# Paired blocks of a GELU feed-forward: where the GELU tiles start, and 512-column products cut in two

## The chip, the cores and the metric

One core of one Trainium2 chip runs the whole program. The metric is device time in microseconds (us). The kernel before takes 477.94 us, the median of 3 runs (477.3 to 478.46). The profiled execution shown below took 477.47 us, of which 475.9 us are the span of its instructions, so 1.57 us lie around the span.

## The reference

A gated linear attention (a state of 48 x 48 per head that decays by alpha and takes up k v at each of 768 steps, for 4 batches and 8 heads) makes x of 3072 tokens by 384. Then comes the feed-forward part, which is all that the change touches:

```
h = x @ w_in                                  # 384 -> 2048
g = 0.5 * h * (1.0 + erf(h * inv_sqrt2))      # GELU
return (g @ w_out).astype(np.float32)         # 2048 -> 384
```

## The kernel before

Every fp32 operand of the feed-forward part is held as two tiles of a shorter format (fp32r), a high part and the rest: `x` (both parts in one tile), `wih`/`wil` of w_in, `woh`/`wol` of w_out, `ghi`/`glo` of the GELU. A product of two fp32 blocks is then three products on TensorE: high by high, high by rest, rest by high. In every one of them the stationary operand is 128 x 128 and loaded anew, and the moving operand has 256, 384 or 512 columns. A matmul row of the trace is one such product.

The tokens go in blocks. While the attention part still runs, blocks are narrow (256 tokens): `gemm1` (L682) has 256 moving columns of `x`, `gemm2` (L918) has 384 moving columns of w_out. Later blocks are wide (512 tokens, `WIDE`): `wide1` (L698) has 512 moving columns of `x` in 9 products for each 128 rows f of w_in's output, `wide2` (L713) has 512 moving columns of `ghi` or `glo`.

In the last three wide blocks most steps are paired (`QUICK`: 7, 8 and 7 pairs, 22 in all). A pair takes two f at once. Its two `wide1` are 18 products of 512 columns. Its second GEMM has two halves:

- `quick1` (L806, by `three_terms`): the last 128 of the 384 outputs directly, 6 products with 512 moving columns of GELU (into `acc[2]`); then three blocks of a 2 x 2 scheme with seven block products in place of eight, each with 256 moving columns of one half of a GELU tile, 9 products.
- `quick2` (also recorded at L806): the other four block products, whose moving operands are combinations of GELU halves, 12 products of 256 columns. The combinations are made by VectorE (DVE) at L790 to L796, split into high and rest by ScalarE (ACT) at L799 and by DVE at L802. The trace names the high tile `qd` and the rest `ad`, after the buffers that they reuse.

The stationary operands of the block products are parts of `woh`/`wol`, or sums and differences of such parts, which lie in reused buffers (`x`, `sums_x`, `sums_kn`, `qd`, `kd` and others in the trace).

ACT makes `ghi` (GELU with the output rounded, L893) and the whole GELU `h` (L898); DVE makes `glo` = h - ghi (L908). The tiles of `ghi` and `glo` come from `gelu_tile`: for every second step of the paired stretch from a ring of two buffers (`own` is None), for the others in turn from a third buffer and from the buffers `ghi_vn`/`glo_vn`.

Where a tile starts in a partition, modulo 256 bytes, is set by constants and by filler tiles (`gap`):

```
GELU_AT, HELD_AT, COMB_AT, WIDE_AT, NARROW_AT = 0, 0, 192, 0, 192
```

So before the change all GELU tiles, all weights, their sums and the wide `x` start at 0 modulo 256; the narrow `x` and the tiles of the combinations at 192. Halves and columns within a tile are whole multiples of 256 bytes further on, so a product's moving and stationary operands keep the start of their tiles modulo 256.

The order of the instructions on each engine is written out by a planner that simulates the engines with the costs in `COST` (`quick1`, `quick2`, `low` and so on). It lets a pair's two `wide1` run before the `quick1` and `quick2` of the pair before it: `quick1` waits for the `glo` of its second step, `quick2` for the rest tile of the combinations.

Of the kernel before, what the change touches and what calls it, by code (L numbers as in the profile page):

```python
# [9 lines left out]
F32R = mybir.dt.float32r  # L10
# [34 lines left out]
    wide1=2.1, wide2=2.07, wpart=1.1, quick1=2.45, quick2=1.42, comb1=0.36, comb3=1.08, chi=0.98, clo=1.2, wsum=0.72, wcomb=0.52, whi=0.52, wlo=0.65, gather=1.7, keep=0.95, evac=1.45, wend0=1.38, wend1=2.76, fsum=0.4, fall=0.2, fout=0.2,  # L45
)
LINE = 256
GELU_AT, HELD_AT, COMB_AT, WIDE_AT, NARROW_AT = 0, 0, 192, 0, 192
ORDER = "0 1 a b c 2 d 3 e f 4 g h i j k 5 l m n o p"


# [1 line left out]
def gla_then_gelu_ffn(ctx: ExitStack, tc: tile.TileContext, q, k, v, alpha, qg, kg, ag, vg, w_in, w_out, out):  # L53
    nc = tc.nc
    B, H, D, S = q.shape
    NF, P, NK, _ = w_in.shape
    DM, DFF = NK * P, NF * P
    NT = B * S
    C = 128
    G = 2 * C  # L60
# [7 lines left out]
    NF2 = NF // 2  # L68
# [10 lines left out]
    def gap(pool, size):  # L79

        if size % LINE:
            n = f"gap{len(gaps)}"
            gaps.append(pool.tile([C, size % LINE // 4], F32, tag=n, bufs=1, name=n))

    const = ctx.enter_context(tc.tile_pool(name="const", bufs=1))
    work = ctx.enter_context(tc.tile_pool(name="work", bufs=3))
    ffn = ctx.enter_context(tc.tile_pool(name="ffn", bufs=2))
# [5 lines left out]
    first = first_cm.__enter__()  # L93
# [27 lines left out]
    W = 2 * G  # L121
# [50 lines left out]
    def data_tile(n, i, dtype=F32):  # L172
        return const.tile([P, NPAIR, G], dtype, tag=f"{n}d{i}", name=f"{n}d{i}")
# [3 lines left out]
    for i in range(NB):  # L177
        vbuf.append(const.tile([P, NCH, HV * D + DR], F32, tag=f"vn{i}", name=f"vn{i}"))
        data.append({})
        for n in "akq":  # L180
            if (n, i) in (("q", 0), ("a", 1)):
                gap(const, (COMB_AT - HELD_AT) * (i == 0))
            data[i][n] = data_tile(n, i)
            if (n, i) == ("a", 1):
                gap(const, HELD_AT - COMB_AT)
# [7 lines left out]
    for half in range(2):  # L193
# [6 lines left out]
            base=0,  # L200
# [1 line left out]
            channel_multiplier=-1,  # L202
        )

    wi_hi, wi_lo, wo_hi, wo_lo = (
        [const.tile([P, 2, DM], F32R, name=f"{n}{f2}") for f2 in range(NF2)] for n in ("wih", "wil", "woh", "wol")
    )

    def gelu_minus(hp, ghi):
        h = hp.rearrange("p a t -> p (a t)")  # L210
        nc.tensor.matmul(h, lhsT=minus, rhs=ghi.rearrange("p a t -> p (a t)"), start=False, stop=True, skip_group_check=True)

    def gelu_rest(hp):
        glo = ffn.tile([P, 2, G], F32R, tag="glo", name="glo")
        nc.scalar.copy(glo, hp)
        return glo

    parts_all = const.tile([P, NSB, 2, DM], F32, name="parts")
    parts = [parts_all[:, i] for i in range(NSB)]
    LONG = NK * 2 * G  # L220

    def long_tile(pool, name, **kw):
        return pool.tile([P, LONG + LINE // 4], F32R, name=name, **kw)

    def narrow_x(t):
        at = (NARROW_AT - HELD_AT) % LINE // 4
        return t[:, at : at + LONG].rearrange("p (n h t) -> p n h t", n=NK, h=2)

    x0_room = long_tile(const, "x0")
    x0 = narrow_x(x0_room)  # L230

# [4 lines left out]
    late = []  # L236
# [339 lines left out]
    def block_of(g):  # L576
        return next((pair for pair in WIDE if g in pair), g)

    later = []

    def x_pool():
        if not later:
            early_cm.__exit__(None, None, None)
            later.append(ctx.enter_context(tc.tile_pool(name="later", bufs=1)))
            gap(later[0], WIDE_AT - GELU_AT)
        return later[0]

    def two_x():
        if len(later) < 2:
            later.append(x_pool().tile([P, 2 * LONG + LINE // 4], F32R, name="two_x"))  # L590
        return later[1]

    def both_x(at):
        at = (at - WIDE_AT) % LINE // 4
        return two_x()[:, at : at + 2 * LONG]

    def x_tiles(g):
        pair = block_of(g)
        if pair == g:
            if g == NSB:  # L600
                x = narrow_x(long_tile(late[0], f"x{g}", tag="xn", bufs=1))
                gap(late[0], WIDE_AT - HELD_AT)
            else:
                x = x0 if g in (0, "s") else both_x(NARROW_AT).rearrange("p (g n h t) -> p g n h t", g=2, n=NK, h=2)[:, g - 1]
            xt[g] = x[:, :, 0], x[:, :, 1]
            return x
        if pair not in xt:
            if pair == WIDE[2]:
                x = both_x(WIDE_AT).rearrange("p (n j h t) -> p n j h t", n=NK, j=2, h=2)
            else:  # L610
                x = late[0].tile([P, NK, 2, 2, G], F32R, tag="xl", name=f"x{g}")
            xt[pair] = x
        h = pair.index(g)
        return xt[pair][:, :, h]
# [189 lines left out]
    def three_terms(to, a, b, start):  # L804
        for n, (x, y) in enumerate(((0, 0), (1, 0), (0, 1))):
            nc.tensor.matmul(to, lhsT=a[x], rhs=b[y], start=(start and n == 0), stop=True, skip_group_check=True)  # L806

    def quick1(f2, acc, gs, first, fresh):
        half = [[[x[:, i] for x in g] for i in range(2)] for g in gs]
        whole = [[x.rearrange("p a t -> p (a t)") for x in g] for g in gs]  # L810
        w = [[[x[:, j, e * P : (e + 1) * P] for x in (wo_hi[f2], wo_lo[f2])] for e in range(3)] for j in range(2)]
        s4 = [x[:, 1] for x in sums[f2]]
        three_terms(acc[2], w[0][2], whole[0], first)
        three_terms(acc[2], w[1][2], whole[1], False)
        three_terms(sbank[:, 0, :G], w[0][0], half[0][0], fresh)
        three_terms(acc[0][:, :G], w[1][0], half[1][0], first)
        three_terms(acc[0][:, G:], s4, half[1][1], False)
# [56 lines left out]

    own_g = {}

    def gelu_tile(n, own):

        if own is None:
            return ffn.tile([P, 2, G], F32R, tag=n, bufs=2, name=n)  # L880
        if (n, own) not in own_g:
            if own:
                i = int(n == "glo")
                t = const.tile([P, NCH, HV * D + DR], F32R, tag=f"vn{i}", name=f"{n}_vn").rearrange("p j e -> p (j e)")
                at = (GELU_AT - (HELD_AT, COMB_AT)[i]) % LINE // 4
                own_g[n, own] = t[:, at : at + W].rearrange("p (a t) -> p a t", a=2)
            else:
                own_g[n, own] = ffn.tile([P, 2, G], F32R, tag=f"{n}3", bufs=1, name=n)
        return own_g[n, own]

    def gelu_high(hp, own=None):
        ghi = gelu_tile("ghi", own)
        nc.scalar.activation(ghi, hp, AF.Gelu)  # L893
        return ghi

    def gelu_whole(hp, half=None):
        h = hp if half is None else work.tile([P, 2, G], F32, tag=("fl", "kx")[half], bufs=1, name="h")
        nc.scalar.activation(h, hp, AF.Gelu)  # L898
        return h

    def gelus(g, f, hp):
        ghi = gelu_high(hp)
        gelu_whole(hp)
        return ghi

    def gelu_low(g, f, hp, ghi, own=None):
        glo = gelu_tile("glo", own)
        nc.vector.tensor_tensor(out=glo, in0=hp, in1=ghi.bitcast(F32), op=ALU.subtract)  # L908
        return glo

# [327 lines left out]

    total = const.tile([P, 1], F32, name="total")
    flag = const.tile([1, 1], I32, name="flag")  # L1240
    gap(const, -64)
    gap(ffn, GELU_AT - HELD_AT)

    def flag_sum():
        nc.vector.tensor_scalar(
# [148 lines left out]
    def gemm1_op(g, t):  # L1394
        f = next_f[g]
        next_f[g] += 1
        st = dict(g=g, f=f, first=g != state["g"], last=False)
# [12 lines left out]
        fast = g in QUICK and f // 2 in QUICK[g]  # L1410
        if fast and not state["more"]:
            assert unit[n_units - 1]["mask"].end is not None and unit[n_units - 1]["mask"].end <= t
            state["more"] = 1
            state["count"] = 0
        own = None
        if state["more"]:
            m = state["count"]
            own = None if m % 2 else m // 2 % 2
            two = steps[-4] if m > 2 else steps[-3] if m == 1 else {}
            state["count"] += 1  # L1420
# [9 lines left out]
            st["gemm1"] = Op("PE", "wide1" if wide else "gemm1", lambda: st.update(hp=(wide1 if wide else gemm1)(g, f)))  # L1430
        past = steps[-2] if fast and "pair" in steps[-2] else None
        room_free = two.get("frees", two.get("gemm2"))
        st["high"] = Op("ACT", "gelu", lambda: st.update(gh=gelu_high(st["hp"], own)), [st["gemm1"], room_free], rank=-3)
        st["gelu"] = Op("ACT", "gelu", lambda: st.update(h=gelu_whole(st["hp"], f % 2 if fast else None)), [st["high"], past and past["low"], past and past.get("c3")], rank=-3)
        if len(steps) < STEPS_BY_PRODUCT:
            st["minus"] = Op("PE", "gminus", lambda: gelu_minus(st["hp"], st["gh"]), [st["gelu"]], rank=-2)
            st["low"] = Op("ACT", "rest", lambda: st.update(gl=gelu_rest(st["hp"])), [st["minus"], room_free], rank=-3)
            waiting["PE"].append(st["minus"])
        else:
            st["low"] = Op("DVE", "low", lambda: st.update(gl=gelu_low(g, f, st["h"], st["gh"], own)), [st["gelu"], room_free], rank=-3)  # L1440

        def second(which):
            if "acc" in st:
# [165 lines left out]
    t = 0.0  # L1609
    idle = 0  # L1610
    while True:
# [17 lines left out]
        t = min(later_on)  # L1629
# [92 lines left out]
```

## Time and profile before

| what | value |
|---|---|
| median of 3 runs | 477.94 us |
| profiled execution | 477.47 us |
| its span | 475.9 us |
| TensorE (PE) busy | 466.1 us, 98% |
| weight loads (PEld) busy | 411.2 us, 86% |
| DVE busy | 340.6 us, 72% |
| ACT busy | 230.6 us, 48% |
| granted TensorE clock | full, mean 0.996 |

PE is busy from about 50 us to its last product at 469.2 us. A matmul row gives the start and a modelled duration, which holds the way through the array; products that follow each other overlap in it. How fast TensorE takes them is therefore read from the distance between starts.

### The profile page before, as it was taken

Reading aid. Unit: us, or ns where it says so; the run is one execution under the profiler, and the core shown is the slowest. Engines: PE = TensorE matmul, PEld = TensorE weight load, DVE = VectorE, ACT = ScalarE, POOL = GpSimd, SP = SyncE. Lnnn points to the kernel's source line nnn. Section 1 sums busy time; section 2 is a strip of 40 time slices with the busy share of each in tenths; the row PEclk is TensorE's granted clock in tenths of the full one; section 3 lists DMA queues with packets and bytes.
Section 4 is the critical chain, followed back from the end, with each engine's and each line's share of the span. In section 5 each row is a group of like instructions: output and inputs, shape, how many; then the busy total and the mean of one; then the engine's idle time right before and its main releaser. Section 6 shows DMA issues by size and latency. Waiting matters only on the chain.

```text
span 475.9 us, 12527 instructions
## 1 busy us (share of the span) xinstructions
PE 466.1 (98%) x5328; PEld 411.2 (86%) x5328; DVE 340.6 (72%) x666; ACT 230.6 (48%) x429; POOL 7.4 (2%) x21
## 2 busy tenths in 40 slices
PE   8999999999999999999999999999999999999994
PEld 5788999999999999887888878888888888888883
DVE  6999999987977978788992365887575454745442
ACT  4898676454544344535433345454444343534340
POOL 2000000000000000000000000000000000000000
PEclk9999999999999999999999999999999999999998
DMA  8997655556756654646340031000010000010002
GB/s 298 401 392 259 234 168 163 165 179 179 213 157 195 209 168 154 205 139 211 117 148 0 22 137 33 1 0 2 0 68 0 1 0 1 23 45 0 1 1 74
DMA packets 33920, 56.67 MB, mean 119 GB/s; under 512 B 3744, under 2 KB 13280, under 8 KB 33856
## 3 DMA queue, kind: packets, MB, share of 16 engines
q1 hardware_dynamic: 32400, 50.94, 32.3%
q0 software_dynamic: 880, 3.93, 2.1%
q8 instruction: 44, 0.72, 0.6%
q10 hardware_dynamic: 576, 0.92, 0.6%
q14 instruction: 20, 0.16, 0.1%
HBM read 43.45 MB, written 12.32 MB: 117 GB/s over the span
## 4 chain that ended last, share of the span: by engine, by line
PE 91%; DMA 4%; DVE 3%; issue 1%; ACT 0%; SPq 0%; DVEq 0%; ACTq 0%
PE hw L698 28%; PE acc L918 13%; PE hp L682 13%; PE accw L806 11%; PE accw L713 9%; PE sbank L806 6%; PE sbank L482 2%; DMA st<-in_moe_w_out_dram 2%; PE sbank L559 2%; PE sbank L501 2%; DMA two_x<-zd 1%; PE sh L392 1%; DVE pp L352 1%; DMA ad<-in_ag_dram 0%; DVE rp L365 0%
## 5 line engine op out<-in xcount | busy, mean ns | idle before, releaser
L698 PE MATMUL hw<-x,wih 128*128 128x512 f32 x288 | 89.2, 391 | 0.0
L893 ACT ACTIVATE ghi<-hw 128x512 fp32r<-128x512 f32 x53 | 31.7, 599 | 70.1 <-PE hw L698 70.1
L698 PEld LDWEIGHTS hw<-x,wih 128*128 128x128 f32 x288 | 52.9, 188 | 10.4
L698 PE MATMUL hw<-x,wil 128*128 128x512 f32 x144 | 56.2, 390 | 0.0
L802 DVE TENSOR_TENSOR ad<-ad,qd 128x1024 fp32r<-128x1024 f32 x22 | 26.9, 1224 | 32.1 <-ACT qd L799 32.1
L799 ACT CAST qd<-ad 128x1024 fp32r<-128x1024 f32 x22 | 23.1, 1051 | 47.3 <-PE accw L806 47.3
L918 PE MATMUL acc<-woh,ghi 128*128 128x384 f32 x128 | 43.9, 343 | 0.0
L918 PE MATMUL acc<-wol,ghi 128*128 128x384 f32 x128 | 43.0, 336 | 0.0
L908 DVE TENSOR_TENSOR glo<-h,ghi 128x512 fp32r<-128x512 f32 x33 | 22.8, 692 | 28.0 <-ACT h L898 28.0
L893 ACT ACTIVATE ghi<-hp 128x512 fp32r<-128x512 f32 x32 | 19.1, 598 | 41.8 <-PE hp L682 41.7
L365 DVE TENSOR_TENSOR_SCAN rp<-ad,rp,bottom 128x255 f32<-128x255 f32 x48 | 34.2, 740 | 0.9
L682 PE MATMUL hp<-two_x,wih 128*128 128x256 f32 x192 | 33.5, 278 | 1.1 <-DMA two_x<-zd 1.1
L682 PE MATMUL hp<-x,wih 128*128 128x256 f32 x192 | 33.9, 279 | 0.0
L352 DVE TENSOR_TENSOR_SCAN pp<-ad,bottom 128x256 f32<-128x256 f32 x48 | 30.7, 668 | 3.4 <-DMA ad<-in_ag_dram 3.4
L698 PEld LDWEIGHTS hw<-x,wil 128*128 128x128 f32 x144 | 27.0, 188 | 5.7
L682 PEld LDWEIGHTS hp<-two_x,wih 128*128 128x128 f32 x192 | 29.5, 188 | 1.2 <-issue 1.2
L698 PE MATMUL hw<-two_x,wih 128*128 128x512 f32 x96 | 29.6, 390 | 0.0
L682 PEld LDWEIGHTS hp<-x,wih 128*128 128x128 f32 x192 | 29.4, 188 | 0.2
L918 PE MATMUL acc<-woh,glo 128*128 128x384 f32 x128 | 28.3, 342 | 0.0
L908 DVE TENSOR_TENSOR glo<-hw,ghi 128x512 fp32r<-128x512 f32 x20 | 13.8, 689 | 20.3 <-ACT hw L898 20.0
L682 PE MATMUL hp<-two_x,wil 128*128 128x256 f32 x96 | 26.6, 277 | 0.0
L682 PE MATMUL hp<-x,wil 128*128 128x256 f32 x96 | 26.4, 277 | 0.0
(282 smaller groups left out, 1120.5 us busy)
## 6 DMA issues: line engine op xcount, KB each, us to landing
st<-in_moe_w_in_dram SPq DMA_DIRECT2D x8, 768.0 KB, 7.4
st<-in_moe_w_out_dram SPq DMA_DIRECT2D x8, 768.0 KB, 6.2
qd<-in_qg_dram SPq DMA_DIRECT2D x23, 256.0 KB, 3.5
ad<-in_ag_dram SPq DMA_DIRECT2D x23, 256.0 KB, 3.3
kd<-in_kg_dram SPq DMA_DIRECT2D x23, 256.0 KB, 4.9
vn<-in_vg_dram SPq DMA_DIRECT2D x12, 416.0 KB, 6.5
fd<-fl SPq DMA_DIRECT2D x18, 256.0 KB, 2.1
kx<-fd SPq DMA_DIRECT2D x72, 64.0 KB, 2.9
```

The costliest lines, as they stand in the source:

```text
L352: nc.vector.tensor_tensor_scan(pp[:, i], at[:, i], bottom, MID, ALU.mult, ALU.max)
L365: nc.vector.tensor_tensor_scan(rp[:, i, G - 2 :: -1], at[:, i, G - 1 : 0 : -1], bottom[:, 1:], rp[:, i, G - 1 :], ALU.mult, ALU.max)
L482: nc.tensor.matmul(ybank[o, i, j * CS : (j + 1) * CS], lhsT=vn[r, j, e : e + rows], rhs=d["ss"][r, h, j, :], start=(j == 0 and i not in sp ...
L682: nc.tensor.matmul(hp[:, j, :], lhsT=a[:, j, i * P : (i + 1) * P], rhs=x[:, i, :], start=(start and m == 0), stop=(stop and (j, i, n) in t ...
L698: nc.tensor.matmul(hp, lhsT=a[:, j, i * P : (i + 1) * P], rhs=x[:, i, :, part], start=(i == 0 and n == 0), stop=(i == NK - 1 and n == 2),)
L713: nc.tensor.matmul(acc[i], lhsT=w[:, j, e], rhs=a, start=(f == 0 and k == 0 and w is wo_hi[f2]), skip_group_check=mixed, stop=(f == NF - 1 ...
L799: nc.scalar.copy(quick["hi"], quick["t"])
L802: nc.vector.tensor_tensor(out=quick["lo"], in0=quick["t"], in1=quick["hi"].bitcast(F32), op=ALU.subtract)
L806: nc.tensor.matmul(to, lhsT=a[x], rhs=b[y], start=(start and n == 0), stop=True, skip_group_check=True)
L893: nc.scalar.activation(ghi, hp, AF.Gelu)
L908: nc.vector.tensor_tensor(out=glo, in0=hp, in1=ghi.bitcast(F32), op=ALU.subtract)
L918: nc.tensor.matmul(acc[t], lhsT=a[:, j, t * C : (t + 1) * C], rhs=w[:, j, :], start=(first and j == 0 and k == 0 and w is wo_hi[f]), stop= ...
```

## The change

GELU tiles of paired steps start at 192 modulo 256 bytes; those of all other steps still start at 0 (`FIRST_GELU_AT`), save where an unpaired step falls to a buffer that only knows the new place (one step at the very end). To this end the ring of two becomes two tiles with a little room, in which a step takes the place it wants. The six products of 512 columns in `quick1` become twelve of 256. Sums of weights stay at 0 modulo 256, and so do the weights of both GEMMs (the fillers are set for it); the buffers that hold sums become 64 bytes shorter. `minus` and `products`, used in a few products at the start, move to 192.

```
-GELU_AT, HELD_AT, COMB_AT, WIDE_AT, NARROW_AT = 0, 0, 192, 0, 192
+GELU_AT, W_IN_AT, WIDE_AT, COMB_AT, HELD_AT, NARROW_AT, FIRST_GELU_AT = 192, 0, 0, 192, 0, 192, 0
...
 def quick1(f2, acc, gs, first, fresh):
     half = [[[x[:, i] for x in g] for i in range(2)] for g in gs]
...
-        three_terms(acc[2], w[0][2], whole[0], first)
-        three_terms(acc[2], w[1][2], whole[1], False)
+        for i in range(2):
+            for j in range(2):
+                three_terms(acc[2][:, i * G : (i + 1) * G], w[j][2], half[j][i], first and i == j == 0)
...
-    def gelu_tile(n, own):
+    def gelu_tile(n, own=None, at=FIRST_GELU_AT):
 
         if own is None:
-            return ffn.tile([P, 2, G], F32R, tag=n, bufs=2, name=n)
+            k = own_g[n] = own_g.get(n, 1) ^ 1
+            base = HELD_AT if n == "ghi" else GELU_AT
+            most = max((x - base) % LINE // 4 for x in (FIRST_GELU_AT, GELU_AT))
+            t = ffn.tile([P, W + most], F32R, tag=f"{n}{k}", bufs=1, name=n)
+            at = (at - base) % LINE // 4
+            return t[:, at : at + W].rearrange("p (a t) -> p a t", a=2)
...
+        at = GELU_AT if fast else FIRST_GELU_AT
...
-        st["high"] = Op("ACT", "gelu", lambda: st.update(gh=gelu_high(st["hp"], own)), [st["gemm1"], room_free], rank=-3)
+        st["high"] = Op("ACT", "gelu", lambda: st.update(gh=gelu_high(st["hp"], own, at)), [st["gemm1"], room_free], rank=-3)
```

The planner's costs and rules are as before, and ACT, DVE, SP and POOL have the same instructions in the same order. Only PE's list differs, in every one of the 22 pairs.

PE before, the second pair's `quick1` from its first product (`accw2` is `acc[2]`, `ghi_vn`/`glo_vn` the GELU of the pair's first step, `ghi`/`glo` of its second, numbers are buffers):

```order
L806 MATMUL accw2_6_4291<-ghi_vn_4463,woh2_136 128x512
L806 MATMUL accw2_6_4291<-ghi_vn_4463,wol2_144 128x512
L806 MATMUL accw2_6_4291<-glo_vn_4469,woh2_136 128x512
L806 MATMUL accw2_6_4291<-ghi_4488,woh2_136 128x512
L806 MATMUL accw2_6_4291<-ghi_4488,wol2_144 128x512
L806 MATMUL accw2_6_4291<-glo_4493,woh2_136 128x512 [waits DVE_49]
L806 MATMUL sbank_80<-ghi_vn_4463,woh2_136 128x256
```

PE now, the same place:

```order
L811 MATMUL accw2_6_4292<-ghi_vn_4465,woh2_136 128x256
L811 MATMUL accw2_6_4292<-ghi_vn_4465,wol2_144 128x256
L811 MATMUL accw2_6_4292<-glo_vn_4471,woh2_136 128x256
L811 MATMUL accw2_6_4292<-ghi_4496,woh2_136 128x256
L811 MATMUL accw2_6_4292<-ghi_4496,wol2_144 128x256
L811 MATMUL accw2_6_4292<-glo_4501,woh2_136 128x256 [waits DVE_49]
```

The six rows now take the first half of each tile, and the same six names follow once more for the second half before `sbank` comes. The wait for DVE's `glo` still stands before the sixth product, which now has only products of 256 columns ahead of it.

PE now, where that pair's `quick1` ends and `quick2` begins (`x0` and `sums_x` hold sums of weights):

```order
L811 MATMUL accw0_6_4290<-ghi_4496,x0_151 128x256
L811 MATMUL accw0_6_4290<-ghi_4496,sums_x_3440 128x256
L811 MATMUL accw0_6_4290<-glo_4501,x0_151 128x256
L811 MATMUL sbank_80<-qd0_4444,x0_151 128x256 [waits Activation_49]
L811 MATMUL sbank_80<-qd0_4444,sums_x_3440 128x256
L811 MATMUL sbank_80<-ad1_4445,x0_151 128x256 [waits DVE_49]
```

These rows stand as they stood before; only the first three read their moving operand from 192 in place of 0.

## Rows read from the trace of the kernel before

**Rows 1.** The page: busy time by engine, PE and its clock in 40 slices
```profile
PE 466.1 (98%) x5328; PEld 411.2 (86%) x5328; DVE 340.6 (72%) x666; ACT 230.6 (48%) x429; POOL 7.4 (2%) x21
...
PE   8999999999999999999999999999999999999994
...
PEclk9999999999999999999999999999999999999998
```

**Rows 2.** Busy time by stretch: stretch, length, then busy us of PE, PEld, DVE...
```profile
195.70:295.40 99.70, 99.70 (x1218) 79.82 (x1218) 66.77 (x148) 43.21 (x88) 1.29 (x2) 1.00 0.35 113
295.40:465.40 170.00, 170.00 (x975) 149.81 (x974) 100.82 (x193) 73.58 (x118) 1.08 (x2) 1.00 0.03 11
```

**Rows 3.** The chain that ended last, paired blocks: start us, length us, what
```profile
299.44 4.09 PE hw L698 x18
303.54 1.36 PE accw L806 x6
...
305.97 1.04 PE sbank L806 x9
...
457.57 4.09 PE hw L698 x18
```

**Rows 4.** Timeline of PE, one pair: start us, duration us, instruction
```profile
437.79 0.39 PE L806 MATMUL accw<-ghi,woh 128*128 128x512 f32 x1
...
438.92 0.39 PE L806 MATMUL accw<-glo,woh 128*128 128x512 f32 x1
439.15 0.28 PE L806 MATMUL sbank<-ghi,woh 128*128 128x256 f32 x1
439.26 0.28 PE L806 MATMUL sbank<-ghi,wol 128*128 128x256 f32 x1
...
440.22 0.40 PE L806 MATMUL sbank<-qd,sums_x 128*128 128x256 f32 x2
...
440.58 0.39 PE L806 MATMUL sbank<-qd,sums_x 128*128 128x256 f32 x2
...
441.60 0.39 PE L698 MATMUL hw<-x,wih 128*128 128x512 f32 x1
```

**Rows 5.** Groups by form, PE: line, names, shapes, count | busy us, mean ns
```profile
L806 PE MATMUL accw<-glo,woh 128*128 128x256 f32 x22 | 6.2, 283 | 0.0
L806 PE MATMUL accw<-qd,woh 128*128 128x256 f32 x22 | 6.1, 276 | 0.0
```

**Rows 6.** The chain again, narrow blocks
```profile
68.68 4.08 PE hp L682 x36
...
89.63 4.17 PE acc L918 x24
```

**Rows 7.** Timeline of PE where a narrow block turns from L918 to L682
```profile
93.63 0.39 PE L682 MATMUL hp<-x,wih 128*128 128x256 f32 x2
93.86 0.28 PE L682 MATMUL hp<-x,wil 128*128 128x256 f32 x1
93.97 0.39 PE L682 MATMUL hp<-x,wih 128*128 128x256 f32 x2
```

**Rows 8.** Timeline of DVE and ACT around the same pair
```profile
431.20 0.69 DVE L908 TENSOR_TENSOR glo<-h,ghi 128x512 fp32r<-128x512 f32 x1 [1.01 <-ACT h L898]
434.90 1.23 DVE L802 TENSOR_TENSOR ad<-ad,qd 128x1024 fp32r<-128x1024 f32 x1 [2.01 <-ACT qd L799]
...
438.48 0.59 ACT L898 ACTIVATE h<-hw 128x512 f32<-128x512 f32 x1
```

**Rows 9.** Timeline of PE behind the last pair: its first and last product
```profile
465.32 0.39 PE L713 MATMUL accw<-ghi,woh 128*128 128x512 f32 x1
...
469.19 0.39 PE L713 MATMUL accw<-glo,woh 128*128 128x512 f32 x1
```

More of the change, by code (lines that the diff above doesn't have):

```diff
@@ L180, in gla_then_gelu_ffn @@
         for n in "akq":
-            if (n, i) in (("q", 0), ("a", 1)):
-                gap(const, (COMB_AT - HELD_AT) * (i == 0))
+            if (n, i) == ("q", 0):
+                gap(const, COMB_AT - HELD_AT)
             data[i][n] = data_tile(n, i)
@@ L203, in gla_then_gelu_ffn, with weight_tiles @@
         )
-    wi_hi, wi_lo, wo_hi, wo_lo = (
-        [const.tile([P, 2, DM], F32R, name=f"{n}{f2}") for f2 in range(NF2)] for n in ("wih", "wil", "woh", "wol")
-    )
+    def weight_tiles(n):
+        return [const.tile([P, 2, DM], F32R, name=f"{n}{f2}") for f2 in range(NF2)]
+    gap(const, W_IN_AT - HELD_AT)
+    wi_hi, wi_lo = weight_tiles("wih"), weight_tiles("wil")
+    gap(const, HELD_AT - W_IN_AT)
+    wo_hi, wo_lo = weight_tiles("woh"), weight_tiles("wol")
     def gelu_minus(hp, ghi):
@@ L213, in gelu_rest @@
     def gelu_rest(hp):
-        glo = ffn.tile([P, 2, G], F32R, tag="glo", name="glo")
+        glo = gelu_tile("glo")
         nc.scalar.copy(glo, hp)
@@ L222, in long_tile @@
     def long_tile(pool, name, **kw):
-        return pool.tile([P, LONG + LINE // 4], F32R, name=name, **kw)
+        return pool.tile([P, LONG + (NARROW_AT - HELD_AT) % LINE // 4], F32R, name=name, **kw)
     def narrow_x(t):
@@ L589, in two_x @@
         if len(later) < 2:
-            later.append(x_pool().tile([P, 2 * LONG + LINE // 4], F32R, name="two_x"))
+            later.append(x_pool().tile([P, 2 * LONG + (NARROW_AT - WIDE_AT) % LINE // 4], F32R, name="two_x"))
         return later[1]
@@ L601, in x_tiles @@
                 x = narrow_x(long_tile(late[0], f"x{g}", tag="xn", bufs=1))
-                gap(late[0], WIDE_AT - HELD_AT)
+                gap(late[0], WIDE_AT - NARROW_AT)
             else:
@@ L887, in gelu_tile, with gelu_high @@
             else:
+                if n == "ghi":
+                    gap(ffn, GELU_AT - HELD_AT)
                 own_g[n, own] = ffn.tile([P, 2, G], F32R, tag=f"{n}3", bufs=1, name=n)
         return own_g[n, own]
-    def gelu_high(hp, own=None):
-        ghi = gelu_tile("ghi", own)
+    def gelu_high(hp, own=None, at=FIRST_GELU_AT):
+        ghi = gelu_tile("ghi", own, at)
         nc.scalar.activation(ghi, hp, AF.Gelu)
@@ L904, in gelus, with gelu_low @@
         return ghi
-    def gelu_low(g, f, hp, ghi, own=None):
-        glo = gelu_tile("glo", own)
+    def gelu_low(g, f, hp, ghi, own=None, at=FIRST_GELU_AT):
+        glo = gelu_tile("glo", own, at)
         nc.vector.tensor_tensor(out=glo, in0=hp, in1=ghi.bitcast(F32), op=ALU.subtract)
@@ L1240, in gla_then_gelu_ffn @@
     flag = const.tile([1, 1], I32, name="flag")
-    gap(const, -64)
-    gap(ffn, GELU_AT - HELD_AT)
+    gap(const, HELD_AT - NARROW_AT - 64)
     def flag_sum():
@@ L1439, in gemm1_op @@
         else:
-            st["low"] = Op("DVE", "low", lambda: st.update(gl=gelu_low(g, f, st["h"], st["gh"], own)), [st["gelu"], room_free], rank=-3)
+            st["low"] = Op("DVE", "low", lambda: st.update(gl=gelu_low(g, f, st["h"], st["gh"], own, at)), [st["gelu"], room_free], rank=-3)
         def second(which):
```

## The prediction

> **What bounds the kernel now.** I read the page's busy times first: PE is busy for 98% of the span at the full clock, and only its first slice is below 9 tenths but for the tail [rows 1]. Then the busy time by stretch: from 295.40 to 465.40, where the 22 pairs run, PE is busy for 170.00 of 170.00 us, DVE for 100.82 and ACT for 73.58 [rows 2]. No wait of PE stands in this stretch. The chain of waits agrees: pair after pair it goes through 18 products at L698 and 27 at L806, all on PE, and nothing of ACT or DVE lies between [rows 3]. So the end is set by how close TensorE takes its products, and an edit is worth what it changes in the distance between their starts.
>
> That distance is read in two ways. One is the chain: from 299.44 to 457.57 lie 20 pairs, 158.13 / 20 = 7.907 us each, of which the 18 products of `wide1` take 4.09 [rows 3]; 3.81 us are left for the second GEMM. The other is the timeline of one pair, from 437.79 to 441.60, again 3.81 us [rows 4]. It falls in four pieces [rows 4]:
>
> - six products of 512 columns, GELU at 0 modulo 256 bytes, 437.79 to 439.15: 1.36 us, 226.7 ns each;
> - nine of 256 columns, GELU at 0, 439.15 to 440.22: 1.07 us. The first, behind a product of 512, takes 0.11 us, so the other eight take 0.96, which is 120 ns each;
> - the first three of 256 columns with a combination at 192, 440.22 to 440.58: 0.36 us, still 120 ns each;
> - the other nine with combinations at 192, 440.58 to 441.60: 1.02 us, 113.3 ns each.
>
> The same shape, 256 columns with a new 128 x 128 stationary operand each time, thus has two prices in one pair. The groups by form say it again: modelled 283 ns where GELU at 0 moves and 276 ns where a combination at 192 moves, both with `woh` as the stationary operand [rows 5]. What differs is the tile that moves, and by its address that is 0 against 192. The narrow blocks give a third witness with other tiles: `x` at 192 by `wih`/`wil`, 36 products in 4.08 us, 113.3 ns each [rows 6].
>
> **The change part by part.**
>
> *Nine products of 256 columns in `quick1`.* Only their moving tile goes from 0 to 192; their stationary operands stay at 0, as those of the nine cheap products are [rows 4]. I take 113.3 ns: 9 x 113.3 = 1.02 us in place of 1.07, so -0.05 us a pair, -1.1 us over 22 pairs. Bounds: the 120 ns they have now (no gain), and 113.3, the least that the trace has for the shape.
>
> *The first three products of `quick2`.* They start at 192 already and cost 120 ns, and from the fourth on the price is 113.3 [rows 4]. I read this as the end of the switch from 0 to 192, and the nine ahead of them will no longer be at 0. The other switch, from 384 columns at 0 to 256 at 192, has no such start: 93.63, 93.86, 93.97 are two products in 0.23 us and a third in 0.11 [rows 7]. So 3 x 113.3 = 0.34 in place of 0.36: -0.02 us a pair, -0.4 us in all. The other end is no gain, if it is the place of their own tile or bank that costs it.
>
> *Six products of 512 into twelve of 256.* Twelve at 192 are 12 x 113.3 = 1.36 us, as much as the six cost now [rows 4]. So this edit is worth nothing, and is needed only since the GELU tile moves: a 512-column product at 192 stands nowhere in the trace of before. If the twelve cost 120 ns, 1.44 us, it loses 0.08 us a pair, 1.8 us in all. Each of the twelve loads weights anew; the narrow blocks show 36 loads in a row at this distance [rows 6], and a pair now has 33 in a row, so no new run is longer than one that is there.
>
> A rule speaks against the cut. The Trainium skill, TensorE: Matmul & The Clock Gate, section Back-to-back issue gap, puts the isolated distance at the columns over 2.4 GHz plus 2.5 ns, and its section Step-by-step: what each phase is for has weights loaded by a read port of their own; neither has a term for where a tile starts. By that rule each cut costs 2.5 ns, an estimate of 6 x 22 x 2.5 ns = 0.33 us more, and moving the tiles gives nothing. The trace does not agree: one shape has two distances, 120 and 113.3 ns [rows 4], both well over the 109.2 ns that the rule would give.
>
> *What lies beside it.* ACT writes `ghi` and DVE reads and writes GELU tiles at the new place. I have no row for these two operations at 192, but they are off the path by far. The `glo` that the pair at 437.79 waits for is done at 431.20 + 0.69 = 431.89, and the sixth product waits for it at 438.92 [rows 4, 8]. With 256-column products ahead of it, it comes 5 x 113.3 ns = 0.57 us in place of 1.13 us behind the first: 6.4 us of cover in place of 7.0. Behind the waiting product stands all of `quick1`, but nothing makes it wait. The combinations' rest tile is done at 434.90 + 1.23 = 436.13, 4.1 us before its first use group at 440.22, and the bank that `wide1` takes at 441.60 is read for the last time at 438.48 + 0.59 = 439.07 [rows 4, 8]. The pair gets shorter by less than 0.1 us, so 2.5 us stay. Even an ACT or DVE operation of twice the length would be hidden. Cost: nothing.
>
> *Behind the pairs.* The next products at L698 come after a switch from 192 to 0, as they do now. Of the 18 products from 465.32 to 469.19 [rows 9] nine read GELU in a buffer that now starts at 192, with 512 columns. From the nearest rows: 120 - 113.3 = 6.7 ns less, or twice that more, 9 products: -0.06 to +0.12 us. I take 0.
>
> *Room and first products.* The wide and narrow blocks keep their places (0 for 384 and 512 columns, 192 for 256). `minus` and `products` at 192 are used in a few products at the start; nothing.
>
> **The sum.** 22 x (0.05 + 0 + 0.02) = 1.5 us; with the unrounded distances, 7.907 - 4.09 - 33 x 0.1133 = 0.078 us a pair from the chain and 3.81 - 3.74 = 0.07 from the timeline, so 1.5 to 1.7. I take 1.55 us. The profiled execution: 475.9 - 1.55 = 474.35 us of span, and with the 1.57 us around it 475.9. It lay 0.47 us under the median; the median becomes 477.94 - 1.55 = 476.4 us.
>
> **The rivals.**
>
> *The start of quick2 stays at 120 ns.* Then only the nine products gain: -1.1 us, 476.8. For it: the three all go to one part of the combinations, the same in every pair. Against it: the other nine products of the combinations have the low price, and so have the first ones behind 384 columns at 0 [rows 4, 7].
>
> *The low price belongs to the tiles, not to the place.* On the other side: if GELU tiles go on moving at 120 ns wherever they start, twelve products cost 1.44 us in place of 1.36, the nine and the three stay, and each pair gets 0.08 us longer: +1.8 us, 479.7. The place is the block at the head of `quick1`. It decides from the distance s at which 21 s + 0.34 equals 1.36 + 1.07 + 0.36, that is 117 ns. For it: no row of before has GELU moving at 192. Against it: `x` by `wih` and combinations by `woh` share nothing but the place, and both have 113.3 [rows 4, 6].
>
> *Place is worth nothing and a cut is free.* The nine then keep their 1.07 us and the twelve take the 1.36 us of the six, whatever makes the combinations cheaper, and the sum is 0 (477.9). The rule named above would add its estimate to that, 478.3. Against it stand the two distances [rows 4].
>
> *That the change does not do what it says* would need a paired step whose tile stays at 0; by `at = GELU_AT if fast` and the three kinds of buffers all 44 steps of the pairs go to 192, so I give it no chance of its own.
>
> **How the numbers follow.** Forecast 80%, the start of `quick2` staying 9%, no effect 5%, the slower case 6%. The three runs of before lie 1.2 us apart, so a median carries some 0.4 us either way. The bound for a difference is 0.2%, 0.96 us here, about what a measurement of this kernel can tell from no change: faster means under 476.98. The forecast lies 0.58 below that and falls there nine times in ten (0.73 of 0.80), the second case somewhat over half of the time (0.06): 0.79 faster. Same: 0.07 + 0.03 + 0.05 = 0.15. Slower: 0.06. The range runs from the best sum, 1.7 + 0.06 us less, by a median's spread to 475.5, and up to 477.4, which holds the second case whole and leaves out the no-effect and the slower case.
>
> **What would show it.** After: 33 products of 256 columns in a row at L811, 113 to 114 ns apart from the first to the last, 3.74 us for all; no 0.12 at the start of `quick2`; a pair in 7.83 to 7.84 us along the chain; 18 products of `wide1` still in 4.09; PE still without waits between the pairs; modelled durations of 276 in place of 283 for the GELU groups. It would be wrong if GELU groups keep 120 ns, if the twelve take longer than 1.38 us, or if PE waits for `glo` at the sixth product.

## The result and the profile after

The changed kernel takes 479.74 us, the median of 8 runs (478.88 to 481.94), against 477.29 us of 8 runs of before on the same chip: a ratio of 1.0051, 95% interval 1.003 to 1.0072. A second comparison on another chip gave 1.0033 (1.0018 to 1.0049), 480.06 against 478.43 us. Both intervals lie above 1: the change makes the kernel slower, by 0.3 to 0.5%. The forecast was 476.4 us, faster.

The bound is where it was. This is the row of the changed kernel's busy time by stretch that answers to [rows 2]: PE is busy through all of the paired blocks, and no wait of PE stands there. The granted clock (the number before the last two) is 1.00 in that stretch, as it was before, so the clock has no part in what follows.

```profile
295.40:465.40 170.00, 170.00 (x1090) 155.04 (x1089) 101.33 (x195) 74.67 (x119) 1.08 (x2) 1.00 0.03 11
```

The chain of the changed kernel, for [rows 3] (start us, length us, what):

```profile
299.40 1.06 PE sbank L811 x9
...
300.82 4.08 PE hw L703 x18
304.89 1.41 PE accw L811 x12
...
460.15 4.08 PE hw L703 x18
```

From 300.82 to 460.15 lie 20 pairs, 7.967 us each in place of 7.907. The twelve cut products take 1.41 us (the six took 1.36 and the forecast was 1.36). And the nine products of `quick2` in `sbank`, which the change does not touch, take 1.06 us where they took 1.04 with three dear ones at their head [rows 3]. The timeline of one pair shows the distances, for [rows 4] (start us, duration us):

```profile
304.73 0.28 PE L811 MATMUL accw<-ghi_vn,woh 128*128 128x256 f32 x1
304.85 0.28 PE L811 MATMUL accw<-ghi_vn,wol 128*128 128x256 f32 x1
...
307.21 0.28 PE L811 MATMUL sbank<-qd,x 128*128 128x256 f32 x1
...
307.56 0.28 PE L811 MATMUL sbank<-qd,x 128*128 128x256 f32 x1
...
308.62 0.61 PE L703 MATMUL hw<-x,wih 128*128 128x512 f32 x2
```

From 304.73 to 308.62 are 33 products in 3.89 us: 117.8 ns each, from the first to the last. The last nine, with the same kind of operands at the same places modulo 256 as before, take 308.62 - 307.56 = 1.06 us, 117.8 ns each, where they took 1.02 us, 113.3 ns [rows 4]. So products that the change does not touch got dearer. The 18 products of `wide1` behind them got a little cheaper (7.967 - 3.887 = 4.080 us in place of 4.095), which takes back 0.3 us over the pairs. The groups by form (for [rows 5]) have one duration for GELU and combinations now, 281 ns, between the 276 and the 283 of before:

```profile
L811 PE MATMUL accw<-glo,woh 128*128 128x256 f32 x88 | 24.7, 281 | 0.0
L811 PE MATMUL accw<-qd,woh 128*128 128x256 f32 x22 | 6.2, 281 | 0.0
```

The narrow blocks, for [rows 6], are as they were, 113.3 ns for the same shape with `x` at 192:

```profile
186.28 4.08 PE hp L687 x36
```

22 pairs by 0.060 us are 1.3 us. The 18 products behind the pairs, nine of them with 512 columns at 192, take 4.18 us in place of 4.11. The chain of before and then of the changed kernel:

```profile
465.48 4.11 PE accw L713 x18
```

```profile
468.12 4.18 PE accw L718 x18
```

Together that is 1.4 us of the 2.45 us between the medians and about all of the 1.6 us on the second chip; the other 1.0 us of the first comparison did not come again, and its interval begins at 1.4 us. The two profiled executions differ by another 1.3 us ahead of the pairs. The comparison of profiles at the end of the experiments shows that such a difference is not a matter of the change.

### The profile page after: what moved, and what is told of

Its sections match the earlier page's. It is cut to its first block, busy times and chain, and to the rows that moved or that the text cites. A ratio compares the mean times of both kernels' runs of the same rounds, so it can differ in the third digit from the quotient of the medians.

```text
span 478.8 us, 12793 instructions
## 1 busy us (share of the span) xinstructions
PE 466.2 (97%) x5460; PEld 417.3 (87%) x5460; DVE 340.1 (71%) x666; ACT 230.0 (48%) x429; POOL 7.4 (2%) x21
## 4 chain that ended last, share of the span: by engine, by line
PE 93%; DVE 3%; DMA 2%; issue 1%; ACT 0%; SPq 0%; DVEq 0%
PE hw L703 27%; PE acc L931 14%; PE hp L687 13%; PE accw L811 11%; PE accw L718 9%; PE sbank L811 6%; PE sbank L487 2%; PE sbank L564 2%; PE sbank L506 2%; DMA two_x<-zd 1%; PE sh L397 1%; DVE pp L357 1%; PE ybank L564 1%; DVE rp L370 1%; PE sbank L397 1%
```

## The experiments

**Theories.** A: a run of 256-column products at 192 has two levels, 113.3 and 117.8 ns; which one it gets is settled where it is entered, and it keeps it. Behind 512 columns it gets the dear one; the second experiment narrowed this to 512 columns at 0. B: the dear level belongs to the long run itself (33 products, each with a new weight load), or to the new places of the tiles. A third question was whether the early buffers that moved cost time.

**The cut alone** (kernel before):

```
-        three_terms(acc[2], w[0][2], whole[0], first)
-        three_terms(acc[2], w[1][2], whole[1], False)
+        for i in range(2):
+            for j in range(2):
+                three_terms(acc[2][:, i * G : (i + 1) * G], w[j][2], half[j][i], first and i == j == 0)
```

> The kernel before with the cut alone: GELU stays at 0, the six products of 512 columns become twelve of 256. Both theories: products at 0 cost 120 ns, so 21 of them 2.51 us, then three at 120 and nine at 113.3 as before; 3.89 us for the second GEMM of a pair, 7.99 us a pair, +1.8 us against before. It shows whether the long run of 256-column products changes the level of the nine last ones (113.3 if the entry from 256 columns at 0 sets it, 118 if the length of the run does).

Measured: 1.0033 (1.002 to 1.0046). Its chain:

```profile
299.69 1.04 PE sbank L806 x9
300.73 0.34 PE accw L806 x3
301.07 4.09 PE hw L698 x18
305.17 1.43 PE accw L806 x12
...
460.80 4.09 PE hw L698 x18
```

The pair takes (460.80 - 301.07) / 20 = 7.987 us, as expected: the cut at 0 costs 1.43 - 1.36 = 0.07 us, and 0.01 us more behind it, where the first of the nine no longer follows a product of 512. That is 13 ns for each of the six cuts. But the run of 33 leaves the last products at their old price, 1.04 and 0.34 us. The length of the run alone does not make them dear.

**The place alone** (changed kernel with the six products whole; the diff is the one above, backwards):

> The changed kernel without the cut: GELU of the pairs at 192, the six products of 512 columns whole. The 512-column products at 192 cost 233 ns (as the nine at the end of the changed kernel do), 1.40 us for six. Theory A (a run of 256-column products at 192 has two levels and keeps the one it is entered in; behind 512 columns it is the dear one): the 21 others 117.8 ns each, 2.47 us, pair 7.97 us, about +1.4 us against before. Theory B (only the long run of 33 is dear): 113.3 ns each, 2.38 us, pair 7.87 us, -0.8 us against before.

Measured: 1.0001 (0.9982 to 1.002). Its chain:

```profile
300.05 4.09 PE hw L703 x18
304.14 1.40 PE accw L811 x6
305.54 0.35 PE sbank L811 x3
305.89 0.68 PE accw L811 x6
...
457.78 4.09 PE hw L703 x18
```

The six cost 233 ns each, and the 21 behind them the low price: three in 0.35 us, six in 0.68 (113.3 ns each). The pair takes 7.887 us. The three dear products at the head stand here behind products at 192, so such a head is no sign of a switch from 0 to 192, which is how the prediction read the three of `quick2`. The expectation that I had put under theory A was wrong, since it took 512 columns at 192 for the same entry as 512 at 0; what theory B expected of the pair, 7.87 us, was near. The new places as such are not dear: GELU at 192 does cost 113.3 ns from the fourth product on, as the prediction said. What is dear is the two edits together.

**Another entry, one more cut** (changed kernel; the last product of the second `wide1` of a pair, 512 columns of `x` at 0, as two of 256 at 0):

```
+                last = i == NK - 1 and n == 2
+                for h in range(2 if last and b in QUICK and f // 2 in QUICK[b] and f % 2 else 1):
+                    ...
+                        hp if whole else hp[:, h],
+                        rhs=x[:, i, :, part] if whole else x[:, i, h, part],
```

> The changed kernel with one more cut: the last product of the second wide1 of each pair (512 columns of x at 0) becomes two of 256 at 0, so that the 33 products are entered from 256 columns at 0 as the twelve of quick2 were before. Theory A (entry decides): two at about 117, three at 120, then 113.3 for thirty: 3.77 us and 0.01 us for the cut, pair 7.87 to 7.88 us, -0.7 us against before, -2 us against the changed kernel. Theory B (the length of the run, or loads of weights that can't be kept up): 117.8 ns all through, pair 7.98 us, +1.6 us against before.

Measured: 0.9986 (0.9972 to 1.0) against before. Its chain (L815 is the second GEMM, L706 `wide1`):

```profile
299.39 4.10 PE hw L706 x19
303.49 1.38 PE accw L815 x12
...
455.23 1.02 PE sbank L815 x9
456.59 4.09 PE hw L706 x18
460.68 1.41 PE accw L815 x12
...
463.16 1.06 PE sbank L815 x9
```

Same places, same 33 products: 1.38 us for the first twelve (three dear ones at the head) and 1.02 for the nine, 7.860 us a pair. The last pair is the control inside the run. The two `wide1` ahead of it belong to steps that are not paired, so nothing is cut there (18 products, not 19), and its twelve take 1.41 us and its nine 1.06: the dear level again. Theory A holds 21 times to one side and once to the other.

**Early buffers back** (changed kernel with `minus`, `products` and two staging buffers at their old places modulo 256):

```
-        return pool.tile([P, LONG + (NARROW_AT - HELD_AT) % LINE // 4], F32R, name=name, **kw)
+        return pool.tile([P, LONG + LINE // 4], F32R, name=name, **kw)
...
+    gap(early, WIDE_AT - GELU_AT)
     products = early.tile([P, (NK + 1) * P], F32R, name="products")
...
```

> The changed kernel with the early buffers where they were before modulo 256 (minus, products and two staging buffers at 0, 0, 0 and 32 in place of 192, 192, 192 and 224; buffers for x and sums with their old length). The pairs are as in the changed kernel: 7.967 us each. If the 1.3 us by which the changed kernel's pairs began later come from these places, they go: about 478.7. If they are chance of one execution, or of the start, the time is that of the changed kernel, 479.7, and the pairs start at another moment in this profile too.

Measured: 1.0022 (1.0007 to 1.0036); the pairs take 7.967 us, as in the changed kernel:

```profile
299.95 4.08 PE hw L704 x18
304.03 1.41 PE accw L812 x12
...
459.28 4.08 PE hw L704 x18
```

The time fits the pairs (1.3 us are 0.28%), so no second cause is needed, though the interval is too wide to exclude one of some 0.4 us. The pairs began at 295.90 us, 0.9 us sooner than in the changed kernel, which taken alone would speak against the early places. The comparison of profiles at the end shows that it is no sign of them.

**An entry from 384 columns** (changed kernel; the product that the third experiment cut in the middle is here cut at column 64 of each half, into one of 128 columns and one of 384):

```
+                cuts = ((0, 64), (64, G)) if last and b in QUICK and f // 2 in QUICK[b] and f % 2 else ((0, G),)
+                for c0, c1 in cuts:
+                    ...
+                        hp[:, :, c0:c1],
+                        rhs=x[:, i, :, part, c0:c1],
```

> The changed kernel; the last product of the second wide1 of each pair (512 columns of x at 0) becomes one of 128 columns and one of 384, both at 0, so the 33 products are entered from 384 columns at 0 as narrow gemm1 mostly is. Theory A (the entry sets the level of the run; behind 512 at 0 it is 117.8 ns): 113.3 ns from the first product on, without the three at 120 that an entry from 256 columns at 0 has: 3.74 us, and about 0.02 us for the cut; pair 7.85 us, -1.2 us against before. Theory C (any further product ahead of the run will do, whatever its columns): lower level too, but with the three dear ones first, 7.86 to 7.87 us. Against both, theory B (the level belongs to the run itself): 117.8, pair 7.98 us.

Measured: 1.0018 (1.0004 to 1.0033), a miss in two terms. Its chain:

```profile
300.63 4.15 PE hw L706 x19
304.78 1.39 PE accw L815 x12
...
459.03 4.09 PE hw L706 x18
463.12 1.41 PE accw L815 x12
```

The cut costs 0.06 us, not 0.02, and the run begins with five products at 117 to 123 ns, though it then goes to 113.3 (and the last pair, uncut, stays dear at 1.41). The clean start that [rows 7] show behind 384 columns is thus no rule. The pair takes 7.92 us.

**One product whole, at the head** (changed kernel; no product ahead of the run is touched):

```
-        for i in range(2):
-            for j in range(2):
-                three_terms(acc[2][:, i * G : (i + 1) * G], w[j][2], half[j][i], first and i == j == 0)
+        g0, (whi, wlo) = half[0], w[0][2]
+        nc.tensor.matmul(acc[2], lhsT=whi, rhs=whole[0][0], start=first, stop=True, skip_group_check=True)
+        for i in range(2):
+            to = acc[2][:, i * G : (i + 1) * G]
+            for x, y in ((wlo, 0), (whi, 1)):
+                nc.tensor.matmul(to, lhsT=x, rhs=g0[i][y], start=False, stop=True, skip_group_check=True)
+        for i in range(2):
+            three_terms(acc[2][:, i * G : (i + 1) * G], w[1][2], half[1][i], False)
```

> The changed kernel with one of the six products left whole: the first product of quick1 has 512 columns of GELU at 192, the other ten of the direct part have 256. Nothing else is cut or moved. Theory A: the run is entered from 512 columns at 192, as in the run with GELU moved and nothing cut, where it had 121.6, 115.8 and 114.2 ns and then 113.3: 0.233 + 31 x 0.1133 + 0.011 = 3.76 us, pair 7.85 us, -1.2 us against before and -2.5 us against the changed kernel. If 512 columns of any place make the run dear when it is long (32 products in place of 21): 0.233 + 31 x 0.1178 = 3.89 us, pair 7.97 us.

Measured: 476.6 us, 0.9968 (0.9952 to 0.9984) against before. Its timeline in a pair:

```profile
304.62 0.39 PE L819 MATMUL accw<-ghi_vn,woh 128*128 128x512 f32 x1
304.85 0.28 PE L823 MATMUL accw<-ghi_vn,wol 128*128 128x256 f32 x1
...
305.20 0.28 PE L823 MATMUL accw<-glo_vn,woh 128*128 128x256 f32 x1
...
308.37 0.63 PE L703 MATMUL hw<-x,wih 128*128 128x512 f32 x2
```

One product of 512 columns at 192 (0.23 us), three to settle (122, 116 and 114 ns), then 28 products from 305.20 to 308.37 in 3.17 us, 113.2 ns each. The pair takes 7.853 us: -1.2 us over the pairs against before, -2.5 against the changed kernel. This is the best version found.

**GELU at 64** (changed kernel, `GELU_AT` 64 in place of 192):

> The changed kernel with the GELU of the pairs at 64 modulo 256 in place of 192; combinations stay at 192. No theory has a row for 64. If the level comes from the switch from 512 columns at 0 to any place but 0: 117 to 118 ns for the 21 GELU products and the twelve behind them, pair 7.97 us. If only the switch from 0 to 192 makes it: 113.3 ns, pair 7.83 us, or 120 ns as at 0, pair 7.99 us.

Measured: 1.0034 (1.0009 to 1.006). Its chain:

```profile
299.41 1.06 PE sbank L811 x9
...
300.82 4.08 PE hw L703 x18
304.90 1.42 PE accw L811 x12
```

The dear level again, for the GELU products at 64 and for the combinations at 192 behind them. A third place for the moving tile, behind the same entry, gives the same price, and the change of place from 64 to 192 inside the run does not end the level. The same products at 64 behind another entry were not tried.

**The direct products last** (kernel before, nothing cut and no tile moved; the two lines for `acc[2]` go behind the other three):

```
-        three_terms(acc[2], w[0][2], whole[0], first)
-        three_terms(acc[2], w[1][2], whole[1], False)
...
         three_terms(acc[0][:, G:], s4, half[1][1], False)
+        three_terms(acc[2], w[0][2], whole[0], first)
+        three_terms(acc[2], w[1][2], whole[1], False)
```

> The kernel before with another order inside quick1: the nine products of 256 columns come first, the six of 512 behind them, so that the twelve of quick2 (at 192 as ever) are entered from 512 columns at 0. No product and no place is changed. Theory A: the twelve go to the dear level, 117.8 ns each, 1.41 us in place of 1.38; the nine behind wide1 at 0 cost 120; pair 7.94 us, +0.7 us against before. If the level of the changed kernel comes from the places of its tiles or from 33 products in a row: 113.3 ns as before, pair 7.89 to 7.91 us.

Measured: 1.0026 (1.0006 to 1.0046). Its chain:

```profile
305.02 2.11 PE accw L806 x12
307.13 1.06 PE sbank L806 x9
```

This is theory A on the kernel before. The same combination products, at the same places, in a run of twelve and not 33, now stand behind 512 columns at 0: the nine take 1.06 us, 117.8 ns each, in place of 113.3. The six of 512 at 0, now behind products of 256, got dearer too (227 to 236 ns; six of 256 and six of 512 take 2.11 us, where 0.72 + 1.36 is the sum of before), which I had not expected; the pair takes 7.953 us, 0.01 more than forecast.

**One product whole, in the midst** (as in "One product whole, at the head", but the whole product is the first of the second step):

```
+        for i in range(2):
+            three_terms(acc[2][:, i * G : (i + 1) * G], w[0][2], half[0][i], first and i == 0)
+        g1, (whi, wlo) = half[1], w[1][2]
+        nc.tensor.matmul(acc[2], lhsT=whi, rhs=whole[1][0], start=False, stop=True, skip_group_check=True)
...
```

> The changed kernel with one product left whole, but in the midst: the six products of the first step are cut as in the changed kernel, the first one of the second step has 512 columns of GELU at 192, the rest is cut. Theory A with a level that any 512-column product at 192 resets: six products at 117.8 ns, one at 233, three behind it at 122, 116 and 114, then 113.4 to the end; 3.79 us, pair 7.88 us, -0.6 us against before. If the level is set once, behind wide1, and stays: 117.8 ns to the end, pair 7.97 us.

Measured: 0.9992 (0.9978 to 1.0005). Its chain:

```profile
312.15 0.71 PE accw L811 x6
312.86 0.23 PE accw L821
313.09 0.47 PE accw L825 x4
313.56 0.34 PE sbank L811 x3
313.90 0.68 PE accw L811 x6
```

Six products at the dear level (0.71 us), one of 512 at 192, and from there the low one (six in 0.68). So the level is not set once per pair: one product of another shape, 512 columns at 192, ended it in the midst of the run.

**The changed kernel and the best version once more, side by side:**

> The changed kernel once more, beside the two others. The pairs take 7.967 us each again, 117.8 ns a product. If the later start of the pairs (296.77 us after the span's start, against 295.47 before) belongs to the kernel, it shows again; if it is chance of one execution, the pairs start at another moment between 295.4 and 297.1 us. Against before +1.3 to +1.5 us by the pairs and the products behind them.

> The version with the first product whole once more, on the same chip as the changed kernel: pair 7.853 us, 2.5 us less than the changed kernel over 22 pairs and 1.2 us less than before. If the gain over before seen on the chip before was chance, the two are level here.

Measured: 1.0033 (1.0018 to 1.0049) for the changed kernel, 0.9981 (0.9966 to 0.9996) for the version with one whole product at the head; 7.967 and 7.853 us a pair again. The chain gives the last narrow block of the best version's two profiles:

```profile
186.28 4.08 PE hp L687 x36
```

```profile
184.53 4.08 PE hp L687 x36
```

One and the same kernel comes to this place 1.75 us sooner in one execution than in another, on another chip. The changed kernel's 1.3 us ahead of its pairs lie within that. Runs on one chip settle it: with the early buffers at the old places the pairs began at 297.02 us (the cut alone) and 295.90 us (early buffers back), with the new places at 296.09 us (the place alone) and 295.47 us (another entry), and before had 295.47 us. The early places do not set the start of the pairs.

The same two profiles show a limit of theory A. Two narrow blocks, each a `gemm1` of 18 products at 192, in the best version's first profile and then in its second:

```profile
59.99 2.04 PE hp L687 x18
63.25 2.12 PE hp L687 x18
```

```profile
58.61 2.12 PE hp L687 x18
61.94 2.06 PE hp L687 x18
```

The kernel is the same and so are the products ahead of each block (384 columns ahead of the first, 128 ahead of the second), yet the first block runs at 113.3 ns once and at 117.8 the other time, and the second block the other way round (its 2.06 us hold a few dearer products at the head). The two profiles come from two chips, but a third one, of the changed kernel on the second chip, with the same code in these blocks, has the levels of the first profile. So the shape and the place of the products ahead fix the level in the pairs, where no wait stands between and every pair repeats the last; they do not fix it everywhere. In the first block, the first product starts 173 ns behind the one ahead of it where the run is cheap and 178 ns where it is dear; that this small shift is the cause was not tested.

## Why the prediction was wrong

*What bounds the kernel:* right. PE has no wait in the paired blocks, and the time went where the distances of products went.

*What lies beside the path:* right. The sixth product came 0.59 us behind the first, in place of 1.13, and did not wait for `glo`: it follows the fifth at the distance of all the others.

*Nine products, 1.07 to 1.02 us:* wrong here, right by itself. With the place alone they reach 113.3 ns from the fourth on, but in the run that was entered behind 512 columns at 0 they cost 117.8, which is 1.06 us.

*The first three of `quick2`, 0.36 to 0.34:* wrong, 0.35, and worse, the nine behind them rose from 1.02 to 1.06 us. For these nine the prediction had no upper bound at all, since the change did not touch them.

*Six into twelve, 1.36 to 1.36:* wrong, 1.41; the upper end for this term, 1.44, held it.

*Behind the pairs:* -0.06 to +0.12 us was the range, and +0.07 us (4.18 in place of 4.11) lies in it; 0 was taken.

The step that failed is one: the price of a shape and a place was taken as a property of the product, with "the least that the trace has", 113.3 ns, for all 33, and the entry into the run was borrowed: "from 384 columns at 0 to 256 at 192, has no such start" was put in the place of an entry from 512 columns at 0, which stands nowhere in the trace of before. The runs show that in the pairs the entry decides the level of the whole run, with 4.5 ns a product between the two: 33 products by 4.5 ns by 22 pairs are 3.3 us, more than twice the forecast gain of 1.55 us, which with the 0.3 us that `wide1` took back became a loss of 1.3 us in the pairs.

The trace of before had the sign. This row of its chain, a narrow `gemm1` behind products of the attention part, is one that I did not read:

```profile
62.37 2.12 PE hp L682 x18
```

18 products at 192 in 2.12 us are 117.8 ns each, with the same code that takes 2.04 us elsewhere ([rows 6] have 113.3 ns for 36). A second level of the same group was in the trace, and it should have been an end of the range. Nor was the clean start behind 384 columns [rows 7] the rule that the prediction took it for: this narrow block of before also stands behind 384 columns and begins with products at 118, 115, 123 and 118 ns.

```profile
87.57 2.06 PE hp L682 x18
```

*The slower rival* gave 479.7 us, which is what was measured, but that is luck. It came by a mechanism that the runs refute, which left GELU at 120 ns and the combinations at 113.3. Both are at 117.8, and GELU alone at 192 is cheap. Its point of decision, 117 ns, was right by arithmetic.

*Place is worth nothing and a cut is free*, the rival of no effect, is refuted too: the place alone took the nine products of `quick1` from 120 to 113.3 ns, and the cut alone cost 0.08 us a pair.

What in the engine sets a level and keeps it is not shown by any run.

## What to carry to other kernels

Where products follow each other without a gap, read the distance of starts by runs and by what stands ahead of each run, not by the shape alone; if one group shows two levels in the trace, or in two profiles of one kernel, both are ends of the range, and products that an edit does not touch can change theirs. After a change of place or width, look first at the first products of the run: one wide product of the new place at the head can be worth more than the cut that removed it.

## What the runs showed of the hardware

All with a new 128 x 128 stationary operand at 0 modulo 256 and fp32r, at the full granted clock. Moving 256 columns at 0 costs 120 ns in a row and 113.3 right behind a product of 512. Moving 256 columns at 192 costs either 113.3 or 117.8 ns; in the pairs the level holds to the end of the run, over up to 33 products, and is the same in all pairs of a profile that have the same entry. Moving 512 columns costs 226.7 ns at 0 and 233 at 192 in a row; at 0 behind products of 256 it cost up to 236 (the direct products last). So at 192 the cheaper level for 256 columns goes with the dearer price for 512.

In the pairs, an entry into 256 columns at 192 from 512 at 0 gave the dear level each time, and one from 256 at 0 or 512 at 192 the low one after three dearer products. In the narrow blocks, the same products ahead gave either level in different profiles.
